# Gate logits as ten more columns of the output weights, in a fused attention and mixture kernel on one core

## The chip, the cores and the metric

The kernel runs on one core of one Trainium2 chip. The metric is the device time of one execution in microseconds (us). Before the change the median of three runs is 615.31 us (613.44 to 615.73). A core has five engines that run side by side and meet at semaphores: TensorE (PE in the profile, its weight loads PEld), VectorE (DVE), ScalarE (ACT), GpSimd (POOL) and SyncE (SP), which issues most DMAs. Each engine executes its own instructions in program order.

## The reference, cut to what matters

```python
a = attention(q, k, v)            # 4 batches, 8 heads, 576 tokens, 64 per head; blocks of 64, causal by block
x = a.reshape(2304, 512)
h = max(x @ w1, x @ w2, x @ w3)   # 768 wide
x = h @ w_out                     # 2304 x 512
# second mixture: top 1 of 8 experts, and a skip
do = x @ w_skip > 0
logits = x @ w_gate               # 8 columns
e = argmax(logits); gate = softmax(logits)[e]
out = x;  out[do] += gate * (relu(x @ w1[e]) @ w2[e])
```

The gate needs nine numbers for each token, `x @ [w_gate, w_skip]`, padded to ten columns. As x is `h @ w_out`, they are also `h @ (w_out @ [w_gate, w_skip])`: the kernel makes the small matrix `w_out @ [w_gate, w_skip]` (768 x 10) itself and multiplies h with it.

## The kernel before, in words

**Tiles.** The 2304 tokens are six chunks of 384 (`CH`), each three tiles of 128. Products with full 32-bit weights are made of two parts: a value is split into a high part (`_h`, type fp32r) and a low part (`_l`), and one product is three: high x high, low x high, high x low. `m_h` (line 725) makes one of 18 hidden products of a chunk: 12 matmuls of 384 columns. `m_y` (line 761) makes the output tile of 128 tokens: 6 blocks of h times 3 parts, so 18 matmuls of 512 columns into one PSUM bank. `m_y_out` (line 775) copies it to SBUF on ACT and `m_y_store` (line 779) sends it to `x2` and `out` by two DMAs.

**Logits.** `m_logits` (line 749) multiplies h with the small matrix `wp` (high and low parts side by side, 20 columns): 12 matmuls of 384 columns whose weights are the 20 columns of `wp`. The result lies the wrong way round (20 x 384): `m_logits_out` (line 757) copies it on ACT and `g_fold` (line 784) turns it and adds the two parts, by one small matmul for each tile. From there go `g_pick` (DVE), `g_exp` (ACT), `g_weight` (DVE), `k_count` (PE), `k_slot` (DVE) and `k_store` (POOL, three scatters of 128 rows into `table`).

**PSUM.** The products `m_h`, `m_y`, `m_logits`, `g_fold` and `k_count` share a ring of two banks (tag `mo`); a bank comes free when its reader on ACT or DVE is done.

**Making `wp`.** `w_out` comes as six pieces of 64-bit words which DVE decodes (`decode`, line 505). Each piece is turned on PE (`wo_turn`), copied on ACT, multiplied with the ten columns (`wo_route`, line 544, 4 matmuls of 10 columns) and split on DVE (`wo_routed`, line 549).

**Order.** For chunks 0 to 4, and for the attention of all chunks, a planner (`Plan`, line 59) sets one order for each engine before anything runs: every task has an engine, a duration, tasks that it waits for, ring buffers that it takes, and `at`, its wish. The planner takes for each engine the task that can start first, and among those within 0.05 the one of the smallest `at`. `build` (line 157) lists the tasks; its chunk loop (lines 312 to 374) has the products, and the attention of the following chunk is interleaved with them. The first hidden product of a chunk waits for the last output product of the chunk before (`prev_y`). After the last attention work, `attention_done` allows the loads of expert weights (`expert_raw`), and `early_row` (line 1103) reads a part of `table` when chunk 4 is stored, for a gather that `first_early` (line 1119) uses in the last chunk.

**Last chunk.** Chunk 5 is written out by hand after the plan (lines 999 to 1037): its hidden products are in the plan, then come `m_logits`, the three `m_y` with small work between their blocks (`mid`), and the expert stage (`Moe2.run`), whose weights stream from HBM. There `T` reuses the room of the output weights and `xe2` holds half rows of one expert.

Of the kernel before, what the change touches and what calls it, by code (L numbers as in the profile page):

```python
# [8 lines left out]
F32 = mybir.dt.float32  # L9
F32R = mybir.dt.float32r  # L10
# [11 lines left out]
P = 128  # L22
# [6 lines left out]
NG = 10  # L29
# [119 lines left out]
def act_time(n, src="psum"):  # L149
    return (0.04 if src == "psum" else 0.09) + 0.83e-3 * n  # L150
# [6 lines left out]
def build(S, E, groups, units):  # L157
# [4 lines left out]
    def later(name, t, *readers):  # L162
        for r in readers:
            r.releases.append((name, t))
# [147 lines left out]
    for c in range(NCH):  # L312
        base = c * span
        rd = {}
        mhs, hls = [], []
        for f in range(NF):
            for i in range(3):
                at = base + (3 * f + i) * 2.1
                deps = piece[3 * f + i] + all_x[c] + (prev_y if f == i == 0 else [])
                mh = S.add("PE", 2.11, at, lambda c=c, f=f, i=i: E.mh(c, f, i), deps, ["mo"])  # L320
                if mhs:
                    mh.deps.append(mhs[-1])
                mhs.append(mh)
                if i == 0:
                    a = S.add("ACT", act_time(CH), at - 1000, lambda c=c, f=f: E.ha(c, f), [mh], ["hm"])
                    later("mo", mh, a)
                else:
                    b = S.add("DVE", dve_time(CH), at - 1000, lambda c=c, f=f, i=i: E.hm(c, f, i), [mh, a], ["hm"])
                    later("mo", mh, b)
                    later("hm", a, b)  # L330
                    a = b
            hh = S.add("ACT", act_time(CH, "sb"), at - 900, lambda c=c, f=f: E.hh(c, f), [a])
            hl = S.add("DVE", dve_time(CH), at - 900, lambda c=c, f=f: E.hl(c, f), [hh])
            later("hm", a, hl)
            hls.append(hl)
        later("x", x_first[c], mhs[-1])
        if c == NCH - 1:
            break
        last_mh = mhs[-1]
        at = base + 38  # L340
        wps = [piece[18 + n][2] for n in range(NF)]
        ml = S.add("PE", 2.11, at, lambda c=c, rd=rd: E.ml(c, rd), hls + wps, ["mo"])
        lt = S.add("ACT", 0.36, at - 1000, lambda c=c, rd=rd: E.lt(c, rd), [ml], ["hm"])
        later("mo", ml, lt)
        ys, stored = [], []
        for t in range(CT):
            y = S.add("PE", 4.12, at + 2 + 4 * t, lambda c=c, t=t: E.my(c, t),
                      hls + [p for n in range(NF) for p in piece[18 + n][:2]], ["mo"])
            if ys:
                y.deps.append(ys[-1])  # L350
            ys.append(y)
            ye = S.add("ACT", act_time(512), at - 500, lambda c=c, t=t: E.ye(c, t), [y], ["y"])
            later("mo", y, ye)
            yd = S.add("SP", 1.2, at - 500, lambda c=c, t=t: E.yd(c, t), [ye], nbytes=2 * 262144)
            later("y", ye, yd)
            stored.append(yd)
        prev_y = [ys[-1], ml]
        g1 = S.add("PE", 0.4, at + 3, lambda c=c, rd=rd: E.g1(c, rd), [lt], ["mo"])
        later("hm", lt, g1)
        g2 = S.add("DVE", 1.3, at - 300, lambda c=c, rd=rd: E.g2(c, rd), [g1, c2])  # L360
        later("mo", g1, g2)
        g3 = S.add("ACT", 0.13, at - 300, lambda c=c, rd=rd: E.g3(c, rd), [g2])
        g4 = S.add("DVE", 0.5, at - 300, lambda c=c, rd=rd: E.g4(c, rd), [g3])
        k1 = S.add("PE", 0.5, at + 7, lambda c=c, rd=rd: E.k1(c, rd), [g4] + ([rk_prev] if rk_prev else []), ["mo"])
        k2 = S.add("DVE", 0.7, at - 300, lambda c=c, rd=rd: E.k2(c, rd), [k1])
        later("mo", k1, k2)
        stored.append(S.add("POOL", 3.0, at - 300, lambda c=c, rd=rd: E.k3(c, rd), [k2]))
        rk_prev = k2
        if c == NCH - 3:
            p1 = S.add("PE", 0.1, at + 8, E.p1, [k2], ["mo"])  # L370
            p2 = S.add("DVE", 1.5, at + 8, E.p2, [p1], ["hm"])
            later("mo", p1, p2)
            later("hm", p2, p2)
            rk_prev = p2
# [71 lines left out]
def _moe1_phase(tc, nc, const, small, g):  # L446
# [12 lines left out]
    with ExitStack() as st_y:  # L459
# [17 lines left out]
            n = 2 * (3 * f + i) + lo  # L477
            return w_all[n // 4][:, n % 4]

        wo = [ypool.tile([P, NF, DM], F32R, tag=n, name=n) for n in ("wo_h", "wo_l")]  # L480
        hid = [ypool.tile([P, NF, CH], F32R, tag=n, name=n) for n in ("h_h", "h_l")]
        mask_q = apool.tile([P, P], BF16, name="mask_q")
        mask_k = apool.tile([P, 64], BF16, name="mask_k")
# [35 lines left out]
        def parts_of(k):  # L519
            c = dec_at[k].bitcast(F32)  # L520
            if k < 18:
                f, i = divmod(k, 3)
                return c.rearrange("p (c f) -> p c f", c=ND), w_piece(f, i, 0), w_piece(f, i, 1)
            return c, wo[0][:, k - 18, :], wo[1][:, k - 18, :]

        def hi_part(k):
            c, hi, lo = parts_of(k)
# [20 lines left out]

        def wo_routed(k):
            f, ps = k - 18, ps_at[k]  # L550
            nc.vector.tensor_copy(wp[:, f, 0:NG], ps)
            nc.vector.tensor_tensor(wp[:, f, NG:2 * NG], ps, wp[:, f, 0:NG], op=ALU.subtract)

        E.raw, E.ab, E.dec, E.hi, E.lo = raw_words, absolute, decode, hi_part, lo_part
        E.tw, E.wt, E.pw, E.wp = wo_turn, wo_turned, wo_route, wo_routed

# [204 lines left out]
        def m_y(c, t, mid=()):  # L761
            ps = my_at[t] = ps_m.tile([P, DM], F32, tag="mo", name="ps_y")
            n = 0
            wo_h, wo_l = wo
            h_h, h_l = hid
            for f in range(NF):
                for at, act in mid:
                    if at == f:
                        act()
                hs = slice(t * P, (t + 1) * P)  # L770
                for a, x in ((h_h, wo_h), (h_l, wo_h), (h_h, wo_l)):
                    nc.tensor.matmul(ps, a[:, f, hs], x[:, f, :], start=(n == 0), stop=(n == 3 * NF - 1))  # L772
                    n += 1

        def m_y_out(c, t):
            y = my_at["y", t] = tmp.tile([P, DM], F32, tag="y", name="y")
# [80 lines left out]
                step(c, rd)  # L857

        E.mh, E.ha, E.hm, E.hh, E.hl = m_h, m_first, m_max, m_hi, m_lo
        E.ml, E.lt, E.my, E.ye, E.yd = m_logits, m_logits_out, m_y, m_y_out, m_y_store  # L860
        E.g1, E.g2, E.g3, E.g4 = g_fold, g_pick, g_exp, g_weight
        E.k1, E.k2, E.k3 = k_count, k_slot, k_store

        def plan_count():
# [177 lines left out]
class Moe2:  # L1042
    def __init__(self, tc, nc, small, ypool, tmp, wpool, xp, ps_m, g):
        self.ps_m = ps_m
        self.tc, self.nc, self.small, self.ypool, self.tmp, self.wpool, self.xp = tc, nc, small, ypool, tmp, wpool, xp
        self.x2, self.table, self.out, self.counts, self.ident = (g[n] for n in ("x2", "table", "out", "counts", "ident"))
        self.order, self.pick, self.two, self.half = (g[n] for n in ("order", "pick", "two", "half"))
        self.m2_w1, self.m2_w2 = g["m2_w1"], g["m2_w2"]
        self.st = ExitStack()
        pool = lambda **kw: self.st.enter_context(tc.tile_pool(**kw))  # L1050
        self.right = pool(name="m2_right", bufs=1, side="right")
        self.raw = [self.right.tile([P, 4, 512], F32, name=f"raw{i}") for i in range(3)]
        self.hi = [self.right.tile([P, 4, 512], F32R, name=f"hi{i}") for i in range(5)]
        self.xg4 = self.right.tile([P, DM], F32, name="xg4")
        self.xe2 = self.right.tile([P, 256], F32, name="xe2")
        self.lo = []
        self.xgs = []
        ps = pool(name="ps_2", bufs=1, space=PSUM)
        self.psa = [ps.tile([P, 512], F32, name=f"psa{i}") for i in range(2)]
        self.pst = [ps.tile([P, 512], F32, name=f"pst{i}") for i in range(2)]  # L1060
        self.psy = [ps.tile([P, DM], F32, name=f"psy{i}") for i in range(2)]
        self.loaded = 0
        self.T = None
        self.eid = []
# [120 lines left out]
    def high_half(self, i):  # L1185

        copy = (self.nc.scalar.copy, self.nc.vector.tensor_copy)[i]
        self.T = self.T or [self.ypool.tile([P, NF, DM], F32R, tag=n, name="T" + n) for n in ("wo_h", "wo_l")]
        r = slice(2 * i, 2 * i + 2)
        copy(self.parts(0)[0][:, r], self.pst[i][:, 0:2 * P].rearrange("p (c t) -> p c t", c=2))  # L1190

# [214 lines left out]
    def index_tables(self):  # L1406
# [2 lines left out]
        self.xo = self.ypool.tile([P, 4, DM], F32, tag="h_l", name="xo")  # L1409
        self.xg2 = self.xo[:, 3]  # L1410
        tb = self.tmp.tile([P, NE, 2, NE], F32, tag="hm", name="tb", bufs=4)
        self.tt = tt = small.tile([P, NE, 2], F32, tag="tt", name="tt", bufs=1)
        self.ti = ti = small.tile([P, NE], I32, tag="ti", name="ti", bufs=1)
        self.tg = tg = small.tile([P, NE], I32, tag="tg", name="tg", bufs=1)
# [157 lines left out]
```

## Time and profile before

| | us |
|---|---|
| median of three runs | 615.31 (613.44 to 615.73) |
| the profiled execution's own time | 618.28 |
| its span, first to last instruction | 616.4 |
| PE busy in the span | 592.0 (96%) |
| DVE busy | 349.0 (57%) |
| ACT busy | 314.8 (51%) |
| granted clock of PE, mean | 0.996 |

The span is what the trace covers; 1.9 us of the profiled execution lie around it. Busy PE time counts overlapping matmuls once; a matmul's recorded length contains its way through the array, so the distance from the start of one to the start of the next, not its length, tells what it costs in a stream. Idle time of an engine that bounds nothing costs nothing. A line such as "L772 PE MATMUL ps_y<-wo_h,h_h 128\*128 128x512" reads: line 772 of the kernel, on TensorE, writes the PSUM tile ps_y from wo_h and h_h, with weights of 128 x 128 and 512 columns streamed.

### The profile page before, as it was taken

How to read it: one execution, taken by the hardware profiler on the slowest of the kernel's cores; microseconds unless marked ns; L12 is line 12 of the kernel's file. 1: busy time of each engine (PE TensorE's matmuls, PEld its weight loads, DVE VectorE, ACT ScalarE, POOL GpSimd, SP SyncE). 2: the span in 40 equal slices, each digit the busy share in tenths (PEclk: the TensorE clock that was granted, in tenths of full speed). 3: DMA queues.
4: the chain of work that ended last, by engine and by line, in shares of the span. 5: the costliest groups of instructions: out<-in, count | busy, mean ns of one | idle time of the engine just before them, and what ended most of it. 6: DMA issues, size and time to landing. Idle time of an engine off the chain costs nothing. (4 is left out here: it accounts for less than half of the span.)

```text
span 616.4 us, 11473 instructions
## 1 busy us (share of the span) xinstructions
PE 592.0 (96%) x4158; PEld 488.1 (79%) x4158; DVE 349.0 (57%) x1007; ACT 314.8 (51%) x814; POOL 44.6 (7%) x101
## 2 busy tenths in 40 slices
PE   6889999999999999999999999999999999899994
PEld 3568798779888888987878887989888997678732
DVE  4899999823555326665265563465542675259600
ACT  4998869933756424545246444436541551158420
POOL 1000000002000010000100001000002002311101
PEclk9999999999999999999999999999999999999998
DMA  6565644421201130102212222100005841799980
GB/s 186 152 201 151 200 155 143 132 90 48 61 28 31 46 106 24 40 20 60 103 39 56 61 76 89 61 22 23 1 6 189 320 153 37 228 364 367 340 286 23
DMA packets 61095, 72.73 MB, mean 118 GB/s; under 512 B 7571, under 2 KB 40597, under 8 KB 61024
## 3 DMA queue, kind: packets, MB, share of 16 engines
q1 hardware_dynamic: 59424, 68.88, 34.8%
q0 software_dynamic: 1600, 2.96, 1.5%
q8 instruction: 38, 0.62, 0.4%
q14 instruction: 33, 0.27, 0.1%
HBM read 61.13 MB, written 11.04 MB: 117 GB/s over the span
## 5 line engine op out<-in xcount | busy, mean ns | idle before, releaser
L731 PE MATMUL ps_h<-x,w 128*128 128x384 f32 x1296 | 243.1, 340 | 0.0
L731 PEld LDWEIGHTS ps_h<-x,w 128*128 128x128 f32 x1296 | 222.6, 188 | 5.9 <-issue 4.7
L651 ACT ACTIVATE p<-sc,nm 128x288 f32<-128x288 f32 (+7 forms) x168 | 84.7, 514 | 27.4 <-DVE nm L640 26.7
L691 ACT COPY pT<-tp 128x512 f32<-128x512 f32 (+2 forms) x106 | 52.2, 505 | 56.8 <-PE tp L686 56.0
L606 PE MATMUL sc<-k,q 64*64 64x288 f32 (+9 forms) x384 | 68.3, 456 | 6.6 <-DMA q<-in_kq_dram 5.0
L686 PE MATMUL tp<-cst_sb,p 128*128 128x128 f32 x432 | 66.0, 282 | 3.9 <-ACT pT L691 1.8
L626 DVE TENSOR_REDUCE nm<-sc 128x2 f32<-128x256 f32 (+7 forms) x64 | 51.5, 813 | 21.8 <-PE sc L613 17.2
L686 PEld LDWEIGHTS tp<-cst_sb,p 128*128 128x128 f32 x432 | 50.0, 143 | 16.6 <-issue 6.9
L705 PE MATMUL pv<-pT,vt 128*64 128x128 f32 (+1 forms) x960 | 60.4, 270 | 1.6 <-ACT pT L691 1.5
L705 PEld LDWEIGHTS pv<-pT,vt 128*64 128x64 f32 x960 | 48.0, 138 | 15.1 <-issue 7.5
L606 PEld LDWEIGHTS sc<-k,q 64*128 64x128 f32 (+1 forms) x384 | 29.8, 180 | 24.2 <-issue 12.3
L672 ACT ACTIVATE p<-p,r 128x512 f32<-128x512 f32 (+8 forms) x74 | 42.9, 597 | 8.8 <-DVE r L666 8.1
L740 DVE TENSOR_TENSOR hm<-ps_h,ha 128x384 f32<-128x384 f32 x36 | 20.0, 556 | 48.1 <-PE ps_h L731 44.1
L772 PE MATMUL ps_y<-wo_h,h_h 128*128 128x512 f32 x108 | 43.8, 406 | 0.0
L772 PE MATMUL ps_y<-wo_l,h_h 128*128 128x512 f32 x108 | 42.3, 391 | 0.0
L772 PE MATMUL ps_y<-wo_h,h_l 128*128 128x512 f32 x108 | 42.2, 390 | 0.0
L777 ACT COPY y<-ps_y 128x512 f32<-128x512 f32 x17 | 9.9, 585 | 53.6 <-PE ps_y L772 46.6
L740 DVE TENSOR_TENSOR hm<-ps_h,hm 128x384 f32<-128x384 f32 x36 | 20.0, 556 | 28.9 <-PE ps_h L731 28.3
L715 ACT CAST x<-pv 128x128 fp32r<-128x128 f32 (+1 forms) x80 | 20.1, 259 | 29.8 <-PE pv L705 29.3
L651 ACT ACTIVATION_READ_ACCUMULATOR p<-sc,nm 128x1 f32 x168 | 34.8, 207 | 0.0
L648 POOL MEMSET p<- 128x128 f32 (+1 forms) x48 | 9.2, 196 | 338.7 <-PE tp L686 220.3
L713 DVE TENSOR_TENSOR x<-pv,x 128x128 fp32r<-128x128 f32 (+1 forms) x80 | 21.2, 275 | 21.1 <-ACT x L715 20.0
(215 smaller groups left out, 741.6 us busy)
## 6 DMA issues: line engine op xcount, KB each, us to landing
raw<-in_m_w_dram SPq DMA_DIRECT2D x19, 1024.0 KB, 6.0
raw<-in_w_dram SPq DMA_DIRECT2D x18, 512.0 KB, 3.8
vt<-in_v_dram SPq DMA_DIRECT2D x16, 320.0 KB, 3.3
x<-y SPq DMA_DIRECT2D x18, 256.0 KB, 2.1
out_dram<-y SPq DMA_DIRECT2D x18, 256.0 KB, 2.3
xa<-in_m_w_dram SPq DMA_DIRECT2D x4, 1024.0 KB
xb<-in_m_w_dram SPq DMA_DIRECT2D x4, 1024.0 KB
raw<-in_w_out_dram SPq DMA_DIRECT2D x6, 512.0 KB
```

The source lines that it names most:

```text
L606: nc.tensor.matmul(bank[:, 0:hi - lo], gd["q"][rows, q0:q0 + nq], gd["k"][rows, lo:hi], start=True, stop=packed or hi != nk)
L626: nc.vector.tensor_reduce(nm, first_ps[:, :, 0:w], axis=AX.X, op=ALU.max, negate=True)
L651: nc.scalar.activation(u["p"][:, j, lo:hi], src, AF.Exp, bias=u["nm"][:, j:j + 1], scale=0.125, accum_out=u["su"][:, n, j:j + 1])
L672: nc.scalar.activation(pt, pt, AF.Copy, scale=r)
L686: nc.tensor.transpose(tp[:, n, :], u["p"][:, j, t * P:(t + 1) * P], ident)
L691: copy(u["pT"][:, m:m + z], u["tp", m][:, 0:z])
L705: nc.tensor.matmul(pv[64 * j:64 * j + 64, 0:nq], vt[:, t, 64 * j:64 * j + 64], pT, start=(t == 0), stop=(t == nkt - 1))
L713: nc.vector.tensor_tensor(xl, pv, xh, op=ALU.subtract)
L715: nc.scalar.copy(xh, pv)
L731: nc.tensor.matmul(ps, a[:, d, :], x[:, d, :], start=(n == 0), stop=(n == 3 * ND - 1))
L740: nc.vector.tensor_tensor(nxt, hm_at["ps", i], hm_at[f], op=ALU.max)
L772: nc.tensor.matmul(ps, a[:, f, hs], x[:, f, :], start=(n == 0), stop=(n == 3 * NF - 1))
```

## The change

In chunks 0 to 4 the small matrix stands as ten more columns behind the 512 columns of the output weights, in one tile `wo_all` (block, high or low, 522 columns). An output tile is made by two products instead of one, of 256 and of 266 columns, each of 18 matmuls; the second one carries the ten gate columns. ACT copies each half (256 columns), DVE copies the ten columns to a small SBUF tile `lg`, and `g_pick` reads that. `m_logits`, `m_logits_out` and `g_fold` are gone from these chunks. The logits of a tile exist only when its second half is done, so `g_pick` and what follows come after the third tile; the wishes of `k_count` and of `plan_count` move from 7 and 8 to 15 and 16. Every output product now also waits for the split gate columns of all six pieces. The last chunk keeps its own logits product; one copy on DVE (`wp_copy`) fills `wp` for it, and its `m_y` reads the first 512 of 522 columns. `T` becomes one tile in the room of `wo_all`, and `xe2` moves into a buffer of the `hm` ring.

```diff
@@ build, chunk loop
         if c == NCH - 1:
+            S.add("DVE", 0.2, base, E.wc, [piece[17 + NF][2]])
             break
         last_mh = mhs[-1]
         at = base + 38
-        wps = [piece[18 + n][2] for n in range(NF)]
-        ml = S.add("PE", 2.11, at, lambda c=c, rd=rd: E.ml(c, rd), hls + wps, ["mo"])
-        lt = S.add("ACT", 0.36, at - 1000, lambda c=c, rd=rd: E.lt(c, rd), [ml], ["hm"])
-        later("mo", ml, lt)
-        ys, stored = [], []
+        ys, stored, gates = [], [], []
         for t in range(CT):
-            y = S.add("PE", 4.12, at + 2 + 4 * t, lambda c=c, t=t: E.my(c, t),
-                      hls + [p for n in range(NF) for p in piece[18 + n][:2]], ["mo"])
...
-            ye = S.add("ACT", act_time(512), at - 500, lambda c=c, t=t: E.ye(c, t), [y], ["y"])
-            later("mo", y, ye)
+            yes = []
+            for j in range(2):
+                y = S.add("PE", (2.16, 2.24)[j], at + 4.4 * t + 2.2 * j, lambda c=c, t=t, j=j: E.my(c, t, j),
+                          hls + [p for n in range(NF) for p in piece[18 + n]], ["mo"])
...
+                yes.append(S.add("ACT", act_time(256), at - 500, lambda c=c, t=t, j=j: E.ye(c, t, j), [y] + yes,
+                                 [] if j else ["y"]))
+                later("mo", y, yes[-1])
+            gates.append(S.add("DVE", 0.08, at - 500, lambda c=c, t=t, rd=rd: E.yg(c, t, rd), [y] + gates[-1:]))
+            later("mo", y, gates[-1])
...
-        prev_y = [ys[-1], ml]
-        g1 = S.add("PE", 0.4, at + 3, lambda c=c, rd=rd: E.g1(c, rd), [lt], ["mo"])
-        later("hm", lt, g1)
-        g2 = S.add("DVE", 1.3, at - 300, lambda c=c, rd=rd: E.g2(c, rd), [g1, c2])
-        later("mo", g1, g2)
+        prev_y = [ys[-1]]
+        g2 = S.add("DVE", 1.3, at - 300, lambda c=c, rd=rd: E.g2(c, rd), [gates[-1], c2])
...
-        k1 = S.add("PE", 0.5, at + 7, lambda c=c, rd=rd: E.k1(c, rd), [g4] + ([rk_prev] if rk_prev else []), ["mo"])
+        k1 = S.add("PE", 0.5, at + 15, lambda c=c, rd=rd: E.k1(c, rd), [g4] + ([rk_prev] if rk_prev else []), ["mo"])
...
-            p1 = S.add("PE", 0.1, at + 8, E.p1, [k2], ["mo"])
-            p2 = S.add("DVE", 1.5, at + 8, E.p2, [p1], ["hm"])
+            p1 = S.add("PE", 0.1, at + 16, E.p1, [k2], ["mo"])
+            p2 = S.add("DVE", 1.5, at + 16, E.p2, [p1], ["hm"])
@@ tiles
-        wo = [ypool.tile([P, NF, DM], F32R, tag=n, name=n) for n in ("wo_h", "wo_l")]
+        wo_all = ypool.tile([P, NF, 2, DM + NG], F32R, tag="wo", name="wo")
+        wo = [wo_all[:, :, n, :] for n in range(2)]
...
-            nc.vector.tensor_copy(wp[:, f, 0:NG], ps)
-            nc.vector.tensor_tensor(wp[:, f, NG:2 * NG], ps, wp[:, f, 0:NG], op=ALU.subtract)
+            hi, lo = (w[:, f, DM:DM + NG] for w in wo)
+            nc.vector.tensor_copy(hi, ps)
+            nc.vector.tensor_tensor(lo, ps, hi, op=ALU.subtract)
+
+        def wp_copy():
+            nc.vector.tensor_copy(wp.rearrange("p f (n g) -> p f n g", n=2), wo_all[:, :, :, DM:DM + NG])
@@ products
-                    nc.tensor.matmul(ps, a[:, f, hs], x[:, f, :], start=(n == 0), stop=(n == 3 * NF - 1))
+                    nc.tensor.matmul(ps, a[:, f, hs], x[:, f, 0:DM], start=(n == 0), stop=(n == 3 * NF - 1))
...
+        def m_y_half(c, t, j):
+            lo, hi = (0, DM // 2) if j == 0 else (DM // 2, DM + NG)
+            ps = my_at[t, j] = ps_m.tile([P, hi - lo], F32, tag="mo", name="ps_y")
+            n = 0
+            for f in range(NF):
+                hs = slice(t * P, (t + 1) * P)
+                for a, x in ((hid[0], wo[0]), (hid[1], wo[0]), (hid[0], wo[1])):
+                    nc.tensor.matmul(ps, a[:, f, hs], x[:, f, lo:hi], start=(n == 0), stop=(n == 3 * NF - 1))
+                    n += 1
+
+        def m_half_out(c, t, j):
+            if j == 0:
+                my_at["y", t] = tmp.tile([P, DM], F32, tag="y", name="y")
+            h = slice(j * DM // 2, (j + 1) * DM // 2)
+            nc.scalar.copy(my_at["y", t][:, h], my_at[t, j][:, 0:DM // 2])
+
+        def m_gates_out(c, t, rd):
+            if t == 0:
+                rd["ps"] = small.tile([P, CT, NG], F32, tag="lg", name="lg", bufs=1)
+            nc.vector.tensor_copy(rd["ps"][:, t, :], my_at[t, 1][:, DM // 2:])
@@ Moe2
-        self.xe2 = self.right.tile([P, 256], F32, name="xe2")
...
-        self.T = self.T or [self.ypool.tile([P, NF, DM], F32R, tag=n, name="T" + n) for n in ("wo_h", "wo_l")]
+        if self.T is None:
+            t = self.ypool.tile([P, 2, NF, DM], F32R, tag="wo", name="T")
+            self.T = [t[:, n] for n in range(2)]
...
+        self.xe2 = self.tmp.tile([P, 256], F32, tag="hm", name="xe2", bufs=4)
```

## Rows read from the trace of the kernel before

**Rows 1.** The page's first part: busy time, share of the span, instructions.

```profile
PE 592.0 (96%) x4158; PEld 488.1 (79%) x4158; DVE 349.0 (57%) x1007; ACT 314.8 (51%) x814; POOL 44.6 (7%) x101
```

**Rows 2.** Busy time of the engines in stretches; the columns are in the first line.

```profile
core 0: us, PE busy (x) PEld busy (x) DVE busy (x) ACT busy (x) POOL busy (x), PEclk, DMA share, GB/s
140.00:215.00 75.00, 75.00 (x581) 65.18 (x579) 35.24 (x92) 40.94 (x111) 4.61 (x13) 1.00 0.14 41
...
440.00:515.00 75.00, 75.00 (x478) 67.43 (x477) 38.95 (x90) 31.59 (x63) 5.35 (x14) 1.00 0.39 137
...
540.00:580.00 40.00, 39.51 (x193) 32.45 (x194) 31.40 (x33) 28.63 (x38) 6.04 (x4) 1.00 0.99 354
```

**Rows 3.** PE timeline, logits and outputs of chunk 4: start, length, line, tiles, count.

```profile
454.27 0.35 PE L754 MATMUL ps_l<-h_h,wp 128*20 128x384 f32 x1
...
456.37 0.39 PE L772 MATMUL ps_y<-wo_h,h_h 128*128 128x512 f32 x1
...
460.46 1.03 PE L686 MATMUL tp<-cst_sb,p 128*128 128x128 f32 x8
461.42 0.83 PE L787 MATMUL ps_r<-cst_sb,lT 20*128 20x10 f32 x6
462.18 0.44 PE L686 MATMUL tp<-cst_sb,p 128*128 128x128 f32 x2
462.38 0.47 PE L772 MATMUL ps_y<-wo_h,h_h 128*128 128x512 f32 x1
...
466.68 1.31 PE L705 MATMUL pv<-pT,vt 128*64 128x128 f32 x20
...
468.17 0.47 PE L772 MATMUL ps_y<-wo_h,h_h 128*128 128x512 f32 x1
...
472.36 37.63 PE L731 MATMUL ps_h<-x,w 128*128 128x384 f32 x216
509.83 0.34 PE L754 MATMUL ps_l<-h_h,wp 128*20 128x384 f32 x1
```

**Rows 4.** Weight loads (PEld): timeline in front of ten-column matmuls, and line 772.

```profile
100.42 0.97 PEld L547 LDWEIGHTS psw<-wr_sb,wt 128*128 128x128 f32 x8 [0.17 <-ACT wo_h L528]
...
L772 PEld LDWEIGHTS ps_y<-wo_h,h_h x108: 186/188/201, 120.8 to 526.6; 128*128 128x128 f32 x108
```

**Rows 5.** PE timeline near the end: matmuls of 256 columns in plain f32.

```profile
604.15 1.90 PE L1322 MATMUL psb<-raw,xo 128*64 128x256 f32 x16
605.88 1.90 PE L1322 MATMUL psb<-xb,xo 128*64 128x256 f32 x16
```

**Rows 6.** Copies out of PSUM, by line: min/median/max ns; one from the ACT timeline.

```profile
L777 ACT COPY y<-ps_y x17: 565/585/588, 125.6 to 522.7; 128x512 f32<-128x512 f32 x17
...
527.76 0.37 ACT L1029 COPY y<-ps_y 128x256 f32<-128x256 f32 x1 [4.45 <-PE ps_y L772]
...
L1030 DVE COPY y<-ps_y x1: 425/425/425, 528.2 to 528.2; 128x256 f32<-128x256 f32 x1
...
L551 DVE CAST wp<-psw x6: 159/162/169, 102.1 to 126.0; 128x10 fp32r<-128x10 f32 x6
```

**Rows 7.** PE timeline, the first output tile of chunk 0 and what follows.

```profile
120.86 0.48 PE L772 MATMUL ps_y<-wo_h,h_h 128*128 128x512 f32 x1
...
125.04 0.95 PE L547 MATMUL psw<-wr_sb,wt 128*128 128x10 f32 x8
...
126.63 0.35 PE L754 MATMUL ps_l<-h_h,wp 128*20 128x384 f32 x1
```

**Rows 8.** From chunk 4's table to its use: timelines of POOL, SP and PE.

```profile
469.41 0.97 POOL L847 DMA_INDIRECT table<-pair,sloti  x1 [26.81 <-DVE cum L844]
...
483.94 0.35 SPq L1105 DMA_DIRECT2D te<-table  x1
...
500.83 1.06 POOL L1115 DMA_INDIRECT xa<-x,ti  x1 [27.36 <-DVE ti L1109]
...
517.41 1.05 PE L1125 MATMUL pst<-cst_sb,xa 128*128 128x128 f32 x8
```

More of the change, by code (lines that the diff above doesn't have):

```diff
@@ L340, in build @@
         at = base + 38
-        wps = [piece[18 + n][2] for n in range(NF)]
-        ml = S.add("PE", 2.11, at, lambda c=c, rd=rd: E.ml(c, rd), hls + wps, ["mo"])
-        lt = S.add("ACT", 0.36, at - 1000, lambda c=c, rd=rd: E.lt(c, rd), [ml], ["hm"])
-        later("mo", ml, lt)
-        ys, stored = [], []
-        for t in range(CT):
-            y = S.add("PE", 4.12, at + 2 + 4 * t, lambda c=c, t=t: E.my(c, t),
-                      hls + [p for n in range(NF) for p in piece[18 + n][:2]], ["mo"])
-            if ys:
-                y.deps.append(ys[-1])
-            ys.append(y)
-            ye = S.add("ACT", act_time(512), at - 500, lambda c=c, t=t: E.ye(c, t), [y], ["y"])
-            later("mo", y, ye)
-            yd = S.add("SP", 1.2, at - 500, lambda c=c, t=t: E.yd(c, t), [ye], nbytes=2 * 262144)
-            later("y", ye, yd)
-            stored.append(yd)
@@ L357, in build @@
-        prev_y = [ys[-1], ml]
-        g1 = S.add("PE", 0.4, at + 3, lambda c=c, rd=rd: E.g1(c, rd), [lt], ["mo"])
-        later("hm", lt, g1)
-        g2 = S.add("DVE", 1.3, at - 300, lambda c=c, rd=rd: E.g2(c, rd), [g1, c2])
-        later("mo", g1, g2)
+        ys, stored, gates = [], [], []
+        for t in range(CT):
+            yes = []
+            for j in range(2):
+                y = S.add("PE", (2.16, 2.24)[j], at + 4.4 * t + 2.2 * j, lambda c=c, t=t, j=j: E.my(c, t, j),
+                          hls + [p for n in range(NF) for p in piece[18 + n]], ["mo"])
+                if ys:
+                    y.deps.append(ys[-1])
+                ys.append(y)
+                yes.append(S.add("ACT", act_time(256), at - 500, lambda c=c, t=t, j=j: E.ye(c, t, j), [y] + yes,
[3 more added lines that the diff above has]
+            later("mo", y, gates[-1])
+            yd = S.add("SP", 1.2, at - 500, lambda c=c, t=t: E.yd(c, t), yes, nbytes=2 * 262144)
+            later("y", yes[0], yd)
+            stored.append(yd)
@@ L523, in parts_of @@
                 return c.rearrange("p (c f) -> p c f", c=ND), w_piece(f, i, 0), w_piece(f, i, 1)
-            return c, wo[0][:, k - 18, :], wo[1][:, k - 18, :]
+            return c, wo[0][:, k - 18, 0:DM], wo[1][:, k - 18, 0:DM]
         def hi_part(k):
@@ L550, in wo_routed @@
             f, ps = k - 18, ps_at[k]
-            nc.vector.tensor_copy(wp[:, f, 0:NG], ps)
-            nc.vector.tensor_tensor(wp[:, f, NG:2 * NG], ps, wp[:, f, 0:NG], op=ALU.subtract)
+            hi, lo = (w[:, f, DM:DM + NG] for w in wo)
[3 more added lines that the diff above has]
+            nc.vector.tensor_copy(wp.rearrange("p f (n g) -> p f n g", n=2), wo_all[:, :, :, DM:DM + NG])
+        E.wc = wp_copy
         E.raw, E.ab, E.dec, E.hi, E.lo = raw_words, absolute, decode, hi_part, lo_part
@@ L859, in _moe1_phase @@
         E.mh, E.ha, E.hm, E.hh, E.hl = m_h, m_first, m_max, m_hi, m_lo
-        E.ml, E.lt, E.my, E.ye, E.yd = m_logits, m_logits_out, m_y, m_y_out, m_y_store
-        E.g1, E.g2, E.g3, E.g4 = g_fold, g_pick, g_exp, g_weight
+        E.my, E.ye, E.yg, E.yd = m_y_half, m_half_out, m_gates_out, m_y_store
+        E.g2, E.g3, E.g4 = g_pick, g_exp, g_weight
         E.k1, E.k2, E.k3 = k_count, k_slot, k_store
```

## The prediction, made before the change was run

> **What bounds the kernel now.** I read the page's first part, then the busy time by stretch, then PE's timeline around one chunk's outputs. PE is busy 592.0 of 616.4 us, the others far less [rows 1]. By stretch, PE has no idle time from 140 to 515: the first and the last of these five stretches of 75 us read 75.00, and the three between read the same, while DVE and ACT are busy about half of the time and DMA a sixth to two fifths [rows 2]. So in chunks 1 to 5 PE sets the pace, and work taken from it there comes off the end. The granted clock is 1.00 in these stretches, the 2.4 GHz level. Only the expert stage is different: from 540 to 580 DMA runs at 0.99 [rows 2].
>
> **What a matmul costs in a stream.** A matmul's recorded length is not its price; the distance between starts is. 216 hidden matmuls of 384 columns run from 472.36 to 509.83, so 173.5 ns each; 18 of 512 columns from 456.37 to 460.46, so 227.2 [rows 3]. Two sizes give a line: 0.42 ns a column and 12.5 ns fixed. The logits product, with weights of only 20 columns, needs 2.10 us for 12, 175 ns each, the same as with 128 columns [rows 3]: at 384 columns the weight load is fully hidden.
>
> **Part 1, removed from PE.** Chunk 4 stands for five: logits product 454.27 to 456.37, 2.10; fold 461.42 to 462.18, 0.76; the three outputs 4.09, 4.30 (462.38 to 466.68) and 4.19 (468.17 to 472.36), together 12.58 [rows 3]. Sum 15.44 us. The first output follows another stream at once; the two that start behind attention or counting work cost 0.1 to 0.2 more, the price of a restart.
>
> **Part 2, added to PE.** Per tile 18 matmuls of 256 columns and 18 of 266. No row has such a matmul in fp32r with 128 columns of weights, so the price is bounded. From the line: 120 and 124 ns. From below, by weight loads: in front of ten-column matmuls, where nothing else can limit, eight loads take 0.97 us; less the length of the last (about 0.19, as in line 772) that is 0.78 / 7 = 111 ns each [rows 4]. A half product needs a load for each matmul, and the load of the next one can only just hide: 111 against 120. From above, two rows: a load's recorded length, 188 ns [rows 4], if all of it came to stand between matmuls; and the plain f32 matmuls of 256 columns, 16 in 1.73 us, 108 ns each with two running side by side on 64 columns of weights, so 216 for one alone [rows 5], if fp32r lost its rate at this size. I take the line, since both points on it are fp32r with the same weights and its value lies above the load's 111. A tile is then 18 x 120 + 18 x 124 = 4.39 us, three 13.18; for restarts I add 0.4, since six products stand where five groups stood and halves that follow each other restart for nothing. 13.6 us. **Gain 15.44 - 13.6 = 1.85 us a chunk, 9.2 in five.**
>
> **A rule that speaks against it.** The Trainium skill, "TensorE: Matmul & The Clock Gate", section "Back-to-back issue gap", gives a stream of load and matmul pairs 81 ns at 128 columns and 131 at 512, paced by both instructions. The trace differs at 512 columns: 227 ns [rows 3]. An estimate on the line through these two figures of the Trainium skill makes a half product's matmul 98 ns, so two cost 65 more than one whole; 270 pairs cost 17.6 us where the removed logits work was 14.3, and the kernel would be 3 us slower. This is the second rival below in its mildest form.
>
> **Part 3, the other engines.** ACT: three copies of 585 ns become six of 370 [rows 6], and the logits copy goes: about equal, and ACT is half idle [rows 2]. DVE: three copies of ten columns, about 0.16 each as the ten-column cast shows [rows 6], and `wp_copy` once; nothing, since DVE has 36 of 75 us free [rows 2]. If that cover failed, it would be 0.5 us a chunk. A bank now has two readers. The last chunk's split copy shows what that does: DVE starts at 528.2, when ACT's copy from 527.76 is through [rows 6]. So a second half's bank may be free 0.2 + 0.37 + 0.2 = 0.8 us after its product; the next taker comes one half product, 2.2 us, later. I cost it at nothing; late next would be that product, by what ACT's queue holds ahead of the copy.
>
> **Part 4, what is moved.** The gate chain starts after the last tile instead of beside it. Its counting matmuls still need a bank, now between hidden products of the next chunk: below nothing is excluded since the count is the same work; up to one drain, 0.4 to 0.8 us a chunk. I take nothing, inside the 0.4 above. In chunk 4 the table is late. From the fold's end at 462.18 to the first scatter at 469.41 are 7.2 us [rows 3, 8], waits included; started at the last output's end instead, the scatter falls 7.2 + 0.5 us behind that end, at about 480 on the old clock, and the last of three at 483. SP reads the table at 483.94 [rows 8], so it waits little; behind it on SP stand expert loads, and the gather that needs it goes at 500.83 and is used at 517.41 [rows 8]: over 15 us of slack. Nothing. POOL does nothing else then. The count of chunk 3 is used a chunk later: nothing. `T` as one tile waits for the whole of `wo_all`, but is written after the last output product in any case, and `xe2` takes a buffer whose last reader is long done: nothing.
>
> **Part 5, chunk 0.** There the first output tile ran from 120.86 to 125.04, and the last piece's gate columns were made after it: their matmuls start at 125.04, and the logits product at 126.63 [rows 7]. Now that tile waits for them. Worst: 126.63 - 120.86 = 5.8 us idle once. But those 1.6 us of PE work have to run anyway and only change places, and attention work of the next chunk can fill. I take 0.5.
>
> **Sum.** 9.2 - 0.5 = 8.7 us. Against the profiled execution: 618.28 - 8.7 = 609.6, span 607.7. It was 3 us above the median; on the median of 615.31 that is **606.6 us**, 1.4% faster.
>
> **The rivals.**
>
> *The order is worse (611).* The planner sorts all tasks anew, and on five engines in fixed order small lateness turns into breaks. For: the breaks are there already, hidden in busy time; the outputs alone hold 0.1 to 0.2 at each restart [rows 3]. Against: shorter products give the planner finer pieces. If three more breaks of 0.3 us a chunk came in, that is 4.5 us: 615.31 - 8.7 + 4.5 = 611. It can go the other way by the same size.
>
> *The half products cost more than half (slower, about 640).* The load of 128 columns comes to stand between matmuls because 256 columns are too short to hide it. Place: line 772's successors, 540 matmuls. For: the spare time is only 9 ns by [rows 4]. Against: the load-limited row itself is below the line's price. Price: each ns above 122 costs 0.54 us; 9.2 / 0.54 = 17, so from a mean of 139 ns the gain is gone, and from 145 it is slower by over 0.5%. At 188 ns: 540 x 66 = 35.6, so 606.6 + 35.6 = 642. The figures of the Trainium skill above, as one case of this, have a chance of 0.02 of the 0.10 I give it.
>
> *The time doesn't come off the end (614).* The change shortens chunks 0 to 4, but the expert stage is paced by DMA [rows 2]. If its loads did not start earlier, it would end when it ended. For: 0.99 DMA. Against: those loads wait for buffers that the last chunk's products free and for the table made in it, so they move with it. 614 to 615.
>
> **Chances.** A measurement of this kernel can tell about 0.5%, 3.1 us, from no change: faster is below 612.2, slower above 618.4. Forecast 0.70 (603.5 to 609.5, all faster); worse order 0.14 (0.08 of it faster, the rest the same); half products too dear 0.10 (slower 0.09, same 0.01); time not off the end 0.06 (same). Faster 0.78, same 0.13, slower 0.09. The range 602 to 613.5 holds the forecast and nearly all of the worse order, some 0.82; below it reaches to a better order, or to 111 ns a matmul, which would give 6 us more than 120 and 124; of the dear half products it holds only their beginning.
>
> **What would show it.** In the new profile: 12 logits matmuls (last chunk) instead of 72; 540 matmuls into ps_y of 256 and 266 columns, starts 120 and 124 ns apart, a tile in 4.4 us; from the logits' place to the next hidden product 13.6 us of PE work a chunk; no idle PE from 140 to some 505; the stage behind the last chunk's products as long as before; table read by SP without delay to the gather. Starts of 139 ns or more, PE waiting for ACT's half copies or DVE's gate copies, or several us of idle PE at chunk 0's outputs would prove it wrong.

## The result and the profile after

The changed kernel takes 608.66 us (median of four runs, 607.55 to 610.22) beside 615.19 for the kernel before on the same chip: ratio 0.9891, interval 0.987 to 0.9912, so 6.5 us or 1.1% faster. Measured again, with more runs, it was 610.38 us beside 617.92, ratio 0.9876 (0.9843 to 0.9909). Forecast were 606.6 us and a gain of 8.7.

The page's first part, which answers to [rows 1]:

```profile
PE 582.6 (96%) x4338; PEld 495.5 (82%) x4338; DVE 349.8 (58%) x1022; ACT 316.7 (52%) x825; POOL 43.3 (7%) x101
```

PE lost 9.4 us of busy time though it runs 180 matmuls more; the other engines kept theirs. From 140 us on PE still has no gap until the last chunk; by stretch, as in [rows 2]:

```profile
140.00:215.00 75.00, 75.00 (x607) 66.93 (x607) 35.72 (x95) 40.51 (x110) 4.35 (x13) 1.00 0.14 39
...
440.00:505.00 65.00, 64.50 (x447) 61.38 (x446) 33.59 (x79) 26.34 (x50) 5.18 (x13) 1.00 0.47 159
```

The outputs of chunk 4 on PE's timeline, which answer to [rows 3] (start, length, line, tiles, count):

```profile
445.62 0.38 PE L787 MATMUL ps_y<-wo,h_h 128*128 128x256 f32 x1
...
450.23 0.28 PE L787 MATMUL ps_y<-wo,h_l 128*128 128x256 f32 x1
...
452.02 0.28 PE L787 MATMUL ps_y<-wo,h_l 128*128 128x256 f32 x1
...
452.26 1.03 PE L691 MATMUL tp<-cst_sb,p 128*128 128x128 f32 x8
453.05 0.37 PE L787 MATMUL ps_y<-wo,h_h 128*128 128x266 f32 x1
453.25 0.28 PE L787 MATMUL ps_y<-wo,h_l 128*128 128x266 f32 x1
...
455.09 0.28 PE L787 MATMUL ps_y<-wo,h_l 128*128 128x266 f32 x1
...
455.34 0.38 PE L691 MATMUL tp<-cst_sb,p 128*128 128x128 f32 x2
455.47 0.36 PE L787 MATMUL ps_y<-wo,h_h 128*128 128x256 f32 x1
...
457.78 1.31 PE L710 MATMUL pv<-pT,vt 128*64 128x128 f32 x20
```

The two rows of 450.23 and 452.02 are 15 matmuls apart: 119 ns each. 453.25 and 455.09 give 123 ns for 266 columns. Three half products in a row run from 445.62 to 452.26, 6.64 us, and each that stands alone restarts once: 2.29 (453.05 to 455.34), 2.31 (455.47 to 457.78) and 2.33 for the last. Together 13.57 us, where the prediction had 13.6 and the old chunk 15.44.

Stage by stage, from PE timelines of two traces of each kernel (us; the second traces are from the first experiments below). The rows that begin a stage in the first traces, where neither [rows 3] nor a row further down shows them, are, before:

```profile
42.16 0.61 PE L731 MATMUL ps_h<-x,w 128*128 128x384 f32 x2
...
511.96 0.40 PE L772 MATMUL ps_y<-wo_h,h_h 128*128 128x512 f32 x1
```

and after:

```profile
41.33 0.44 PE L736 MATMUL ps_h<-x,w 128*128 128x384 f32 x1
...
502.08 0.39 PE L777 MATMUL ps_y<-wo,h_h 128*128 128x512 f32 x1
```

| stage | before | before, again | after | after, again |
|---|---|---|---|---|
| start to the first hidden product | 42.2 | 41.0 | 41.3 | 42.0 |
| from there to the first of chunk 5 | 430.2 | 430.2 | 420.0 | 420.0 |
| from there to the first output of chunk 5 | 39.6 | 39.6 | 40.7 | 40.7 |
| from there to the end | 104.5 | 104.2 | 105.0 | 105.2 |

So 10.2 us are won in chunks 0 to 4, the same in both pairs (0.24 of them because chunk 4's count now runs one stage later); 1.1 us are given back in the last chunk and some 0.8 behind it. The 1.1 is the same in both pairs; the 0.8 is less sure, since the last stage takes from 101.7 to 105.8 us in the traces of the changed kernel and its variants below. What remains is 8.3 us by this sum. The medians say 6.5 and 7.5, with intervals of some 1.3 and 2 us to each side; the start alone differs by 1 us between traces of one kernel.

### The profile page after: what moved, and what is told of

Same layout as the page of the kernel before. It is cut to its first block, busy times and chain, and to the rows that moved or that the text cites. A ratio compares the mean times of both kernels' runs of the same rounds, so it can differ in the third digit from the quotient of the medians.

```text
span 607.1 us, 11847 instructions
## 1 busy us (share of the span) xinstructions
PE 582.6 (96%) x4338; PEld 495.5 (82%) x4338; DVE 349.8 (58%) x1022; ACT 316.7 (52%) x825; POOL 43.3 (7%) x101
## 5 line engine op out<-in xcount | busy, mean ns | idle before, releaser
L787 PE MATMUL ps_y<-wo,h_h 128*128 128x256 f32 (+1 forms) x360 | 68.8, 287 | 0.0
L787 PEld LDWEIGHTS ps_y<-wo,h_h 128*128 128x128 f32 x360 | 56.7, 189 | 1.2 <-issue 1.2
L787 PE MATMUL ps_y<-wo,h_l 128*128 128x256 f32 (+1 forms) x180 | 51.1, 284 | 0.0
L677 ACT ACTIVATE p<-p,r 128x576 f32<-128x576 f32 (+8 forms) x73 | 42.3, 596 | 9.0 <-DVE r L671 8.3
L787 PEld LDWEIGHTS ps_y<-wo,h_l 128*128 128x128 f32 x180 | 34.0, 189 | 0.0
L749 ACT CAST h_h<-hm 128x384 fp32r<-128x384 f32 x36 | 18.5, 515 | 28.0 <-DVE hm L745 27.9
```

The lines of the kernel that those rows point to most:

```text
L677: nc.scalar.activation(pt, pt, AF.Copy, scale=r)
L787: nc.tensor.matmul(ps, a[:, f, hs], x[:, f, lo:hi], start=(n == 0), stop=(n == 3 * NF - 1))
```

## The experiments

### The spread, and the two parts of the change

**The kernel before and the changed kernel, again.** No edit.

> The kernel before, unchanged, for a second trace and the spread. The first trace of it had a span of 616.4 us, its execution 618.28 us, 3 us over the median. Theory (the first trace was a slow one in some part that has nothing to do with the change, so the real gain is about 6.5 us and not the 9.3 that the two spans show): a span near 613, and the missing 3 us in one stretch, at the start or in the expert stage. Rival (it is a constant kernel and the spread is in the launch around it): span 616 again, ratio 1.000 either way.

617.94 us, ratio 1.0003 (0.9983 to 1.0022), span 615.0. One microsecond of the difference between the two traces lies ahead of the first hidden product (42.2 against 41.0); the rest of the table agrees within 0.3. No stretch holds the 3 us, so my theory fell, and what put the first execution 3 us above its median is open.

> The changed kernel, unchanged, for a narrower interval and a second trace. Theory: ratio 0.987 to 0.991 to the kernel before (6 to 8 us), products of 256 and 266 columns again about 121 and 124 ns from start to start. Rival (the first four runs were lucky or unlucky by more than 1 us): ratio below 0.986 or above 0.992.

610.38 us, ratio 0.9876 (0.9843 to 0.9909). As expected, and the stages repeat.

**The split alone.** On the kernel before:

```diff
-            y = S.add("PE", 4.12, at + 2 + 4 * t, lambda c=c, t=t: E.my(c, t), ...
+            for j in range(2):
+                y = S.add("PE", 2.16, at + 2 + 4.4 * t + 2.2 * j, lambda c=c, t=t, j=j: E.my(c, t, j), ...
...
+                    nc.tensor.matmul(ps, a[:, f, hs], x[:, f, cols], start=(n == 0), stop=(n == 3 * NF - 1))
...
```

> The kernel before with one thing: each output tile of chunks 0 to 4 as two products of 256 and 256 columns; the logits product, the fold and their order stay. Theory (a matmul costs 12.5 ns and 0.42 ns a column, the weight load just hides): a tile takes 18 x 2 x 120 = 4.32 us instead of 4.09, 0.23 x 15 = 3.5 us slower, ratio 1.006. Rival 1 (halving costs more than this, the load shows): 139 ns a matmul and more, 10 us slower, ratio 1.016. Rival 2 (shorter pieces give the planner a better order, and that is where a part of the gain is): no slower than before, ratio 1.000 or less.

621.38 us, ratio 1.006 (1.004 to 1.0079): 3.5 us slower, what the line gives. The split by itself costs, and no better order comes with it. On its PE timeline, 17 matmuls apart:

```profile
459.25 0.28 PE L785 MATMUL ps_y<-wo_h,h_h 128*128 128x256 f32 x1
...
461.28 0.28 PE L785 MATMUL ps_y<-wo_l,h_h 128*128 128x256 f32 x1
```

119 ns: half of 227 plus 6. The stage from the first hidden product of chunk 0 to that of chunk 5 agrees with the time: 433.8 us instead of 430.2.

```profile
42.05 1.14 PE L734 MATMUL ps_h<-x,w 128*128 128x384 f32 x5
...
475.82 2.42 PE L734 MATMUL ps_h<-x,w 128*128 128x384 f32 x13
```

**The logits product put back** in the changed kernel, as work that nobody uses:

```diff
+        ml = S.add("PE", 2.11, at - 1, lambda c=c, rd=rd: E.ml(c, rd), hls + [wc], ["mo"])
+        lt = S.add("ACT", 0.36, at - 1000, lambda c=c, rd=rd: E.lt(c, rd), [ml], ["hm"])
...
+        g1 = S.add("PE", 0.4, at + 3, lambda c=c, rd=rd: E.g1(c, rd), [lt], ["mo"])
...
+        gd = S.add("DVE", 0.1, at - 300, lambda c=c, rd=rd: E.gd(c, rd), [g1])
...
```

> The changed kernel with the logits product, its copy and its fold put back in chunks 0 to 4 as work whose result nobody uses (the gate still takes the ten columns). Theory (what left PE came off the end one for one): 12 x 175 ns and 0.76 us, with two restarts 3.1 us a chunk, so 14 to 15 us above the changed kernel, about 623, ratio to the kernel before 1.012 to 1.014. Rival (a part of the logits work was filling waits, at the end of a chunk above all): 8 us or less above the changed kernel, ratio 1.002 or less.

623.58 us, ratio 1.0095 (1.006 to 1.0129): 13.2 us above the changed kernel by the medians, below the theory's 14 to 15, as is the ratio below its 1.012 to 1.014, and far above the rival's 8. The trace tells it better, since the stages behind chunk 4 vary on their own. From the first hidden product of chunk 0 to that of chunk 5 it took 434.8 us, and 420.0 in the changed kernel:

```profile
42.16 1.14 PE L744 MATMUL ps_h<-x,w 128*128 128x384 f32 x5
...
476.92 1.75 PE L744 MATMUL ps_h<-x,w 128*128 128x384 f32 x9
```

That is 14.7 us, the theory's figure: the rows' own 2.10 + 0.76 = 2.86 a chunk, without restarts, is 14.3, so none of this work was filling waits. The two experiments close the account of chunks 0 to 4: 14.7 saved, 3.6 paid for the split, 270 x 4 ns = 1.1 for ten more columns leave 10.0, against a measured 10.2.

### Is the weight load the floor?

**192 and 330 columns** instead of 256 and 266:

```diff
-            lo, hi = (0, DM // 2) if j == 0 else (DM // 2, DM + NG)
+            lo, hi = (0, 192) if j == 0 else (192, DM + NG)
...
```

> The changed kernel with its output products of 192 and 330 columns instead of 256 and 266. By the line of 12.5 ns and 0.42 ns a column 192 columns would take 93 ns and the time would stay. Theory (a load of 128 columns of weights needs 111 ns and sets the floor): about 112 and 151 ns, 4.73 us a tile instead of 4.39, 5 us slower than the changed kernel, ratio to the kernel before 0.995 to 0.997. Rival 1 (no floor): 93 ns, ratio 0.988. Rival 2 (under 256 columns fp32r falls to half its rate or less): 172 ns or more for the narrow ones, 20 us slower at least, ratio 1.02 and more.

614.58 us, ratio 0.9958 (0.9933 to 0.9983), in the middle of the theory's range. PE's timeline of it, each pair 15 matmuls apart:

```profile
450.12 0.27 PE L787 MATMUL ps_y<-wo,h_l 128*128 128x192 f32 x1
...
451.80 0.28 PE L787 MATMUL ps_y<-wo,h_l 128*128 128x192 f32 x1
...
452.20 0.32 PE L787 MATMUL ps_y<-wo,h_l 128*128 128x330 f32 x1
...
454.48 0.32 PE L787 MATMUL ps_y<-wo,h_l 128*128 128x330 f32 x1
```

112 ns for 192 columns, where the line without a floor gives 93, and 152 for 330. So there is a floor, and it agrees with the spacing of loads that [rows 4] shows, 111 ns; that it is the load, and not something else in a pair of load and matmul, is read from this agreement and was not tested apart. It holds for these 32-bit weights: the count's nine bf16 matmuls, each with a load of 128 columns too, start 26 ns apart (465.55 to 465.76 below). fp32r has not lost its rate at 192 columns, at least not beyond what the floor covers. The change's 256 columns lie 7 ns above the floor.

### What was given back

**The count in a bank of its own.** The last stretch before the last chunk's table, on the changed kernel's PE timeline:

```profile
461.35 4.35 PE L736 MATMUL ps_h<-x,w 128*128 128x384 f32 x24
465.55 0.18 PE L855 MATMUL ps_k<-cum,ones 128*128 128x8 bf16 x1
...
465.76 0.17 PE L858 MATMUL ps_k<-oh,tri 128*128 128x8 bf16 x1
466.43 0.79 PE L736 MATMUL ps_h<-x,w 128*128 128x384 f32 x3 [0.50 <-DVE hm L745]
```

Chunk 4's count now stands behind two hidden products of chunk 5, takes one of two banks, and PE waits until DVE has drained the other, that is, has read it so that it can be written again. Before, the count stood ahead of the third output, and the 216 matmuls of chunk 5's hidden products ran without a break [rows 3]:

```profile
467.93 0.18 PE L829 MATMUL ps_k<-cum,ones 128*128 128x8 bf16 x1
```

The experiment gives it another bank. It also makes the count wait for the end of the attention work; the count still runs behind the same 24 hidden matmuls:

```diff
+    k1.deps.append(go)
...
+            if c == NCH - 2:
+                ps = m2[0].psy[1][:, 0:CT * NE].rearrange("p (t e) -> p t e", t=CT)
...
```

> The changed kernel with the counting matmuls of chunk 4 in a PSUM bank of their own instead of one of the two of the ring. Theory (in the last chunk, where no attention work is left, they take the bank that the next hidden product needs, and PE waits for VectorE to drain the other): from the first hidden product of chunk 5 to its first output product 39.9 us instead of 40.7, the gain about 0.8 us. Rival (PE waits there because VectorE is late with the gate chain, whatever the bank): still 40.5 or more.

610.32 us, ratio 0.9879 (0.9843 to 0.9914), which can't tell it from the changed kernel. The trace can: from the first hidden product of chunk 5 to its first output 40.0 us instead of 40.7, and the wait is gone:

```profile
461.10 4.35 PE L740 MATMUL ps_h<-x,w 128*128 128x384 f32 x24
465.29 0.18 PE L863 MATMUL psy<-cum,ones 128*128 128x8 bf16 x1
...
465.53 33.54 PE L740 MATMUL ps_h<-x,w 128*128 128x384 f32 x192
```

Of the 1.1 us, 0.7 was the bank; the count's own 0.24 us lies now inside this stage, and some 0.2 are left.

**Loads of code beside a read of the table.** The expert stage needs one half of `T` from DVE. In DVE's order that copy stands behind the making of the index tables, which waits for the read of the whole `table` (8 KB in pieces of 8 bytes). DVE's timeline of the changed kernel:

```profile
522.18 0.29 DVE L1443 TENSOR_TENSOR tb<-te,pick 128x128 f32<-128x128 f32 x1 [3.31 <-DMA te<-table]
...
522.98 0.42 DVE L1217 CAST T<-pst 128x256 fp32r<-128x256 f32 x1
```

The copy itself uses nothing of the read, and PE had made its input by 519.8; putting it ahead of the index tables was not tried. PE's waits for it, for the kernel before and for the changed one (engine, line, who was late: us, times, longest):

```profile
PE psa L1217 <- DVE Two_h L1190: 1.4, 1, 1.4
```

```profile
PE psa L1244 <- DVE T L1217: 2.5, 1, 2.5
```

The DMA view of the window of that read, before and after (queue: packets, MB, share; then the read with its us from issue to landing):

```profile
q1 hardware_dynamic: 1970, 1.80, 94.1%
...
te<-table SPq DMA_DIRECT2D x1, 8.0 KB, 5.8
```

```profile
q1 hardware_dynamic: 2115, 1.98, 84.8%
q8 instruction: 1, 0.02, 0.8%
q14 instruction: 2, 0.02, 0.6%
...
te<-table SPq DMA_DIRECT2D x1, 8.0 KB, 7.3
```

Three loads of the program's own code, one of 16 KB and two of 8 KB, fall into the read after the change and none before. The instructions per chunk have changed, and the theory is that with them the times have moved at which an engine needs its next piece of code. The first experiment moves the large one by 64 more instructions at PE's start:

```diff
+            early = ps_m.tile([P, CT, NE], F32, tag="mo", name="early")
+            for n in range(32):
+                nc.tensor.matmul(early[:, 0, :], mask_q, mask_k[:, 0:NE], start=(n == 0), stop=(n == 31))
```

> The changed kernel with 32 matmuls of 8 columns put ahead of everything on PE, while PE waits for its first data: 64 more instructions in PE's program, so that every later load of its code falls some 5 to 10 us earlier. In both traces of the changed kernel one such load of 16 KB runs while the last read of the table is under way, and that read takes 7.1 to 7.3 us from issue instead of 5.8, with PE waiting behind it. Theory (the load of code delays the read): the read is back at 5.8 us, PE waits 1.4 us for the turned rows instead of 2.5, and from the first output product of the last chunk to the end it takes 104.2 instead of 105.2 us. Rival (the read is late because the expert loads or the stores of the outputs lie otherwise): the read still takes 7 us.

608.34 us, ratio 0.9847 (0.9817 to 0.9877). The read's window:

```profile
q1 hardware_dynamic: 2136, 1.98, 93.6%
q14 instruction: 2, 0.02, 0.6%
...
te<-table SPq DMA_DIRECT2D x1, 8.0 KB, 6.6
```

And PE's wait:

```profile
PE psa L1247 <- DVE T L1220: 2.1, 1, 2.1
```

Half right: without the large load the read is 0.6 us shorter and PE waits 2.1 us, not the theory's 1.4, and the two small ones are still there. From the first output product to the end it took 104.5 us, not 104.2. Two more runs go on from here. The first has the bank and the 64 instructions together:

> The changed kernel with both repairs: the counting matmuls of chunk 4 in a bank of their own, and 64 early instructions on PE that move its code loads. Theory (the two losses are separate and lie one after the other on PE's way): from the first hidden product of chunk 5 to its first output product 40.0 us, from there to the end 104.5, together 1.3 us less than the changed kernel; ratio to the kernel before 0.984 to 0.987, to the changed kernel 0.998. Rival (the expert stage ends when its loads end, so what is won in the last chunk is lost again): over 105.5 us behind the first output product.

605.94 us, ratio 0.9837 (0.9809 to 0.9865), the lowest of this study. The stages: 40.0 and 104.9 us in the profiled execution (at 608.75 us the longest of its six), 0.4 more behind the last chunk than the theory said and less than the rival's 105.5. The read took 6.3 us with the two small loads beside it, and PE waited 1.7 us. Its interval overlaps that of the changed kernel, so by time alone it is not shown to be faster; by the trace the last chunk's 0.7 us is. The second moves the small loads too, by early work on DVE and ACT:

```diff
+            for n in range(16):
+                nc.vector.memset(warm[:, 1:2], 0.0)
+            for n in range(16):
+                nc.scalar.copy(warm[:, 0:1], warm[:, 1:2])
```

> The same with 16 small writes on VectorE and 16 small copies on ScalarE added at the start, where both wait for data: their code loads move too. With the PE load alone moved, the last read of the table took 6.6 us, with two loads of 8 KB still beside it; in the kernel before, with none, 5.8. Theory (each code load beside it costs the read some of its time): if the two loads of 8 KB fall elsewhere, the read takes 5.8 to 6.0 us and PE waits 1.4 to 1.6 us for the turned rows. Rival (the rest has another cause): 6.5 us or more although no code load runs beside it. The time itself: 0.5 us less than with both repairs at best, not to be told by the rounds; the extra work at the start could cost up to 3 us if ScalarE is not idle there.

606.5 us, ratio 0.9845 (0.9815 to 0.9874): not to be told from the one before. The read's window has no code load, the read is even shorter than the theory's 5.8 to 6.0, and PE's wait is back at the old length:

```profile
q1 hardware_dynamic: 1965, 1.78, 103.8%
...
te<-table SPq DMA_DIRECT2D x1, 8.0 KB, 5.2
```

```profile
PE psa L1259 <- DVE T L1232: 1.4, 1, 1.4
```

With no code load beside it the read took 5.8, 5.8 and 5.2 us (the two traces of the kernel before, and this one); with one of 8 KB, in the run with the logits product put back, 6.5; with two of 8 KB 6.6 and 6.3; with these and the one of 16 KB 7.3, 7.1, 7.1, 6.9 and 7.2. Moving the loads moved the read and PE's wait each time (2.5, 2.1, 1.7 and 1.4 us): this cause is shown, though the cost does not grow with each load. What it is worth at the end is not: in the traces this last stage took 101.7 us here and 102.9 with the narrow products, where the read was late, so its end varies by more than the read does.

**Rows of 528 columns.** In the last chunk a matmul of 512 columns takes about 232 ns after the change and 227 before, from start to start, 0.2 us in all.

```diff
-        wo_all = ypool.tile([P, NF, 2, DM + NG], F32R, tag="wo", name="wo")
+        wo_all = ypool.tile([P, NF, 2, DM + 16], F32R, tag="wo", name="wo")
```

> The changed kernel with rows of 528 instead of 522 columns in the tile of the output weights, so that each row begins at a multiple of 64 bytes again. Theory (in the last chunk the matmuls of 512 columns take 232 ns instead of 228 because their rows begin at odd addresses): 228 again there, 0.2 us in all, which the time can't show. Rival (it is the one tile instead of two): 232 still.

610.03 us, ratio 0.9866 (0.9826 to 0.9905), and still about 232 ns. It isn't where the rows begin. Whether it is the one tile instead of two was not tried; the cause is open.

## Why the prediction was right

**What bounds it.** Right: chunks 0 to 4 were PE's, and what the change took from PE there, 10.7 us by the sum that follows, came off the start of chunk 5 nearly one for one (10.2).

**Removed and added.** Right within about a tenth: 9.2 us forecast for the five chunks, 10.2 seen. Added up from start to start, logits and fold were 14.6 us in five chunks (forecast 14.3) and the outputs grew by 3.9 (forecast 5.1): chunk 4, which stood for all, is one of the cheapest in outputs before (12.58, mean 12.65) and the dearest after (13.57, mean 13.43). The line through 384 and 512 columns gave 120 and 124 ns; 119 and 123 were measured. The lower bound, 111 ns, proved to be a real floor, and close. The rule of the Trainium skill ("TensorE: Matmul & The Clock Gate", section "Back-to-back issue gap"), from which the prediction's estimate made the change lose 3 us, does not hold for these matmuls: two halves cost 238 ns where one whole costs 227, and the split alone cost 3.5 us, not the 17.6 of that estimate.

**Chunk 0.** The 0.5 us were not paid. The first output started at 122.2 instead of 120.9 and the outputs ran on without a break; from the first hidden product of chunk 0 to that of chunk 1 it took 94.6 us instead of 97.0. The work that had stood between the outputs only changed places, as the prediction held likely.

**The other engines.** Right. The gate copy on DVE waits for ACT's copy of the same bank, as assumed (ACT's and DVE's timeline behind the last output of chunk 4):

```profile
461.55 0.37 ACT L794 COPY y<-ps_y 128x256 f32<-128x256 f32 x1 [2.15 <-PE ps_y L787]
```

```profile
461.96 0.17 DVE L799 COPY lg<-ps_y 128x10 f32<-128x10 f32 x1 [2.23 <-ACT y L794]
```

0.8 us after the product the bank is free, and no output product waited for it.

**What is moved: the step that failed.** "I take nothing, inside the 0.4 above": the count between hidden products cost one drain, 0.7 us, once, in the chunk that has no attention work to put in between. The bounds of 0.4 to 0.8 were right; they belonged into the sum for the last chunk. The count's own 0.24 us only went from chunk 4's stage to the last chunk's. "SP reads the table ... so it waits little" was wrong: the planner moved the read ahead of an expert load, and it waited 9.6 us for the scatters. SP's waits in the changed kernel (us in all, count, longest):

```profile
SPq L1130 <- DMA table<-pair,sloti: 9.6, 1, 9.6
```

SP's timeline of the same kernel (start and duration in us), where the read goes out only then:

```profile
475.45 0.34 SPq L1130 DMA_DIRECT2D te<-table  x1
```

The expert load behind it went at 476.77, 15.4 us after the chunk's first hidden product instead of 10.9 us before the change. That this costs anything was not shown: no wait of PE on an expert load came with it. I had fixed the read's place by the old order, although the order is made anew.

**What was not thought of.** The late read of the table in the expert stage, up to 1.1 us of PE's wait, by code loads that the new instruction counts moved. Whether the end came later by it is not shown.

**Sum.** 9.2 and 0.5 became 10.2 and 0; 0 for the end became some 1.9 (0.7 the drain, 0.24 the count that moved, some 0.2 open in the last chunk, 0.8 in the last stage, which varies by more than this). By the stages 8.3 us, forecast 8.7; by the medians 6.5 and 7.5. That 8.3 lies so near to 8.7 is in part luck: 1.5 us more than forecast in chunks 0 to 4 and 1.9 that were not forecast nearly cancel. Of the rivals, the worse order was in part what came, in the last chunk and not as breaks everywhere; dear half products and a time that does not come off the end did not come.

## What to carry to other kernels

Where one engine has no gap for hundreds of microseconds, price a change by start-to-start distances of that engine alone, and take the price of a new size from a line through two sizes of the same kind, with the weight load's own spacing as the floor. Ten more columns on a product that runs anyway were far cheaper than a second product (1.1 us against 14.7), even with 3.6 us for the split that made room for them. Then look where the cover ends: the same small insertion that other work hides in the chunks before costs a full drain in the one chunk that runs alone.

## What the runs showed of the hardware that I had not expected

Loads of the program's own code go over the same DMA engines, at places that the instruction counts set. Three of them made a read of 8 KB in pieces of 8 bytes take 7.3 us instead of 5.8, and PE wait 2.5 us behind it instead of 1.4; 64 instructions more on PE, in a time when it waits, moved one of them away. And a stream of fp32r matmuls, each with a load of 128 columns of weights, has a floor of 112 ns a matmul, the spacing of the loads themselves (111): 192 columns cost nearly what 256 do (112 against 119 ns). The bf16 matmuls of the count, with as many columns of weights, start 26 ns apart.
